# Key-value products of two pairs in one unbroken row of 40 matmuls, and their loads two pairs at a time

## The chip, the cores and the metric

The kernel runs on one core of a Trainium2 chip. The metric is the device time of one execution in microseconds (us), taken as the median of several runs. The granted TensorE clock of the profiled execution is 0.997 of full speed over the whole span.

## What is computed

The reference is a linear attention followed by a gated feed-forward layer, for 8 batches, 8 heads of 64 columns and 576 rows:

```python
kv = np.einsum('bhsd,bhse->bhde', k, v)            # 64 x 64 for each batch and head
out = np.einsum('bhsd,bhde->bhse', q, kv)
rms = np.sqrt(np.mean(out * out, axis=-1, keepdims=True) + 1e-06)
x = out / rms * g_norm                              # heads side by side: 576 x 512
...
h = np.maximum(x @ w_in, 0.0)                       # 576 x 1024, halves u and v
v_n = (v - mu) / np.sqrt(var + 1e-06)
v_s = np.einsum('ts,bsd->btd', w_spatial, v_n) + b_spatial[None, :, None]
out = (u * v_s) @ w_out
```

## The kernel before

Two heads make a pair, so a batch has four pairs (`NP = 4`). For each pair `att_k` makes the key-value product: the 576 rows are four chunks of 128 and a tail of 64 (`NC + 1 = 5`), and for each chunk there is one matmul for either head, whose 64 x 64 result goes to its own half of the partitions. That is a row of 10 matmuls in full fp32. The trace records an fp32 matmul twice, so the row has 20 records there. Each pair has a PSUM tile `pskv` of its own from the pool `ps_att` (three banks). VectorE copies the result of the one head, ScalarE that of the other, into `KVB[p % 2]` (even batches) or `KVO[p]` (odd batches).

The keys and values of a pair lie in one of two buffers, `KV[0]` and `KV[1]`, with the tails in `KT`. `att_load` orders these loads on SyncE's queue, and a buffer is loaded anew when the products that read it are done. The queries (`qt`) and the last 128 queries of odd batches (`qs`) have two buffers each.

`att_q` multiplies four chunks of queries by the pair's `kv` (four matmuls `pso`) and normalizes; the tail rows of all pairs collect in `pst` (`att_end`). `att_t` transposes (`pstr`, for the tail `pstt`), and the result is split in a high and a low fp32r part, `XH` and `XL`.

The feed-forward part of a batch then runs as long streams of fp32r matmuls with three products for each operand pair: `psh` (512 columns), `psu` (288 columns), `psa`, `psb` and `psc` (the spatial product, 288 columns) and `pso2` (the output, 512 columns; the trace drops the digit and calls it `pso`, line 272). Batch 0 and the weights are prepared at the start by the order that is written out in `PLAN`, with plain fp32 products (`L355`, `L379`, `L388`). From batch 2 on, `att_steps` gives a list of attention steps, and the functions `first`, `second` and `last` take one step of it after every piece of feed-forward work of the batch before; the scheduler then places the instructions of each engine.

In `att_steps` the steps of an even batch are `K[0], K[1], Q[0], K[2], Q[1], T[0], K[3], ...` and those of an odd batch begin with `K[0], K[1], K[2], K[3]`.

Of the kernel before, what the change touches and what calls it, by code (L numbers as in the profile page):

```python
# [8 lines left out]
F32 = mybir.dt.float32  # L9
# [7 lines left out]
B, H, S, D = 8, 8, 576, 64  # L17
DM, FF = 512, 1024
FH = FF // 2
P = 128  # L20
NP = H // 2
NC = S // P
# [3 lines left out]
NT = NC * P  # L26
# [6 lines left out]
NB = B  # L33
PLAN = """
N8 W L J00 n6 D00 L n8 W G J01 n6 B00 C A01 L n6 W L J02 T00 H00 H10 D02 C H20 H30 B01 W C J03 T01 Z H01 H11 D03 H21 H31 W C
W B02 L T02 H02 H12 H22 H32 W B03 C W d0 T03 H03 H13 H23 H33 b0 e0 e1 e2 e3 C L K10 C t0 L K11 C
u00 u01 u02 u03 F0 L K12 F1 W W L K13 F2 W W W W d1 b1 F3 u10 Q0 u11 X0 u12 L A10 X1 u13 t1 X2 L B10 A11 h X3
T10 s L B11 E0 T11 s A12 s L B12 E1 z s T12 A13 X4 W s B13 L X5 Q1 s T13 X6 L s X7 s P O0 O1 p R W
"""

# [6 lines left out]
def body(ctx: ExitStack, tc, qT, kvm, kvt, g2, w_in, wsT, bsp, w_out, out):  # L47
    nc = tc.nc
# [11 lines left out]
    def persistent(shape, dt, name):  # L60
        return const.tile(shape, dt, name=name, tag=name)
# [21 lines left out]
    TA = [persistent([P, FH + HF], F32R, f"TA{i}") for i in range(2)]  # L83
    TB = [persistent([P, FH + HF], F32R, f"TB{i}") for i in range(2)]
    U = persistent([P, 4, S], F32, "U")
    KVB = [persistent([P, P], F32, f"KVB{i}") for i in range(2)]
    KVO = [persistent([P, P], F32, f"KVO{i}") for i in range(NP)]


    KV = [persistent([P, 2, NC, P], F32, f"KV{i}") for i in range(2)]  # L90
# [9 lines left out]
    keys, queries = {}, {}  # L100
    n_load = [0]

    def att_load(b, p, kind):
        if kind in "fk":
            kv, kt = (x[n_load[0] % 2] for x in (KV, KT))
            n_load[0] += 1
            for i, j in ((0, 2), (2, NC)) if (b, p) == (0, 0) else ((0, NC),):
                nc.sync.dma_start(kv[:, :, i:j], kvm[b, p, :, :, i:j])
            nc.sync.dma_start(kt[0:TAIL], kvt[b, p])
            keys[b, p] = kv, kt, None  # L110
        if kind == "k":
            qs = load.tile([P, P], F32, name="qs", tag="qs")
            nc.sync.dma_start(qs, qT[b, p, :, S - P:S])
            keys[b, p] = kv, kt, qs
        else:
            n = S if kind == "f" else NT
            qt = load.tile([P, S], F32, name="qt", tag="qt")
            nc.sync.dma_start(qt[:, 0:n], qT[b, p, :, 0:n])
            queries[b, p] = qt

    def att_k(b, p, st, copy=nc.vector.tensor_copy):
        kv, kt, qs = keys.pop((b, p))
        ps = ps_att.tile([P, 512], F32, name="pskv", tag="att")

        for c in range(NC + 1):
            of = kv[:, :, c] if c < NC else kt
            for h in slice(0, D), slice(D, P):
                nc.tensor.matmul(ps[h, h], of[:, 0, h], of[:, 1, h],  # L128
                                 start=c == 0, stop=c == NC)
        st[p] = KVO[p] if b % 2 else KVB[p % 2]  # L130
        copy(st[p][0:D, 0:D], ps[0:D, 0:D])
        nc.scalar.copy(st[p][D:P, D:P], ps[D:P, D:P])
        if qs is not None:
            att_end(p, st, qs)
        issue()

    def att_end(p, st, q):

        if p == 0:
            st["tail"] = ps_tail.tile([P, 512], F32, name="pst", tag="tail")  # L140
        nc.tensor.matmul(st["tail"][:, p * P:(p + 1) * P], q, st[p], start=True, stop=True)  # L141
# [23 lines left out]
    def norm_a(ps, rows=P, accumulate=False):  # L165
        x = work.tile([P, 512], F32, name="x", tag="x")[0:rows]
        ss = small.tile([P, 8], F32, name="ss", tag="ss")[0:rows]
        if accumulate:
            for h in range(8):
                cols = slice(h * D, (h + 1) * D)  # L170
                nc.scalar.activation(x[:, cols], ps[0:rows, cols], AF.Square,
                                     accum_out=ss[:, h:h + 1])
        else:
            nc.scalar.activation(x, ps[0:rows], AF.Square)  # L174
            nc.vector.tensor_reduce(ss, heads(x), axis=AX.X, op=ALU.add)  # L175
        return ps, x, rows, rsqrt_a(ss, 8, rows, 1.0 / D, "h")
# [7 lines left out]
    def att_qa(b, p, st, accumulate=False):  # L184
        qt = queries.pop((b, p))
        ps = ps_att.tile([P, 512], F32, name="pso", tag="att")
        for c in range(NC):
            nc.tensor.matmul(ps[:, c * P:(c + 1) * P], qt[:, c * P:(c + 1) * P], st[p],  # L188
                             start=True, stop=True)
        if b % 2 == 0:  # L190
            att_end(p, st, qt[:, S - P:S])
        issue()
        st[p] = norm_a(ps, P, accumulate)

    def att_qb(b, p, st):
        st[p] = norm_b(*st[p])

    def att_q(b, p, st):
        att_qa(b, p, st)
        att_qb(b, p, st)  # L200

    def tail_a(b, st, accumulate=False):
        st["xt"] = norm_a(st["tail"], P, accumulate)

    def tail_b(b, st):
        st["xt"] = norm_b(*st["xt"])
# [35 lines left out]
    def att_steps(b):  # L242

        st = states.setdefault(b, {})

        def loading(f):
            return lambda: (f(), ahead())

        def t2():
            att_t(b, 2, st)  # L250
            tail_a(b, st)
            tail_b(b, st)

        def tail():
            tail_a(b, st)
            tail_b(b, st)

        K = [lambda p=p: att_k(b, p, st) for p in range(NP)]
        Q = [loading(lambda p=p: att_q(b, p, st)) for p in range(NP)]
        T = [lambda p=p: att_t(b, p, st) for p in range(NP)]  # L260
        end = lambda: att_tail(b, st)
        if b % 2 == 0:
            return [K[0], K[1], Q[0], K[2], Q[1], T[0], K[3], Q[2], T[1], Q[3], t2, T[3], end], []
        return [loading(k) for k in K] + [tail, end], [Q[0], Q[1], T[0], Q[2], T[1], Q[3], T[2],
                                                       T[3], move_tail]


    def three(ps, pairs):
# [135 lines left out]
    def product(ps, q, n, of, start=True, stop=True):  # L404


        cols = slice(q * P, (q + 1) * P)
        pairs = [m for k in range(2) for m in hl(VH[:, k, n, cols], VL[:, k, n, cols],
                                                 WSH[:, k, of], WSL[:, k, of])]
        for i, (lt, rh) in enumerate(pairs):  # L410
            nc.tensor.matmul(ps, lt, rh, start=start and i == 0, stop=stop and i == len(pairs) - 1,  # L411
                             skip_group_check=True)
# [195 lines left out]
    def split_tail():  # L608
# [10 lines left out]
        for n in (TAIL, r):  # L619
            keep(nc.scalar.copy(WTL[1][n - TAIL:n - TAIL + 1], f32(WTL[0][n:n + 1])))  # L620

    todo = [(b + (kind != "f"), p, kind) for b in range(0, B, 2) for kind in "fkq"
            for p in range(NP)]
    states = {}
    wanted = [0]

    def issue():

        while wanted[0] and todo and (len(queries) if todo[0][2] == "q" else len(keys)) < 2:
            wanted[0] -= 1  # L630
            att_load(*todo.pop(0))

    def ahead(n=1):
        wanted[0] += n
        issue()

    nc.vector.memset(KVB[1], 0.0)
    nc.vector.memset(epsc, EPS)
    nc.scalar.activation(small.tile([P, 1], F32, name="warm", tag="av"), epsc, AF.Sqrt)
    nc.gpsimd.memset(KVB[0], 0.0)  # L640
    for kt in KT:
        nc.gpsimd.memset(kt[TAIL:P], 0.0)
    for kvb in KVO:
        nc.gpsimd.memset(kvb, 0.0)
    make_identity(nc, ident)

    def warm(n):

        ps = ps_tail.tile([P, 512], F32, name="psw", tag="tail")
        for _ in range(n):  # L650
            nc.tensor.matmul(ps[:, 0:P], KVB[1], KVB[1], start=True, stop=True)

    def filler(n):
        for _ in range(n):
            tc.keep_in_program_order(
                nc.tensor.matmul(psv[3][:, 0:P], KVB[1], KVB[1], start=True, stop=True))  # L656

    queue = []

# [15 lines left out]
    def outw():  # L675
# [12 lines left out]
    psv = [ps_mm.tile([P, 512], F32, name="psh", tag="mm") for _ in range(NC)]  # L688
    st = [states.setdefault(b, {}) for b in range(2)]
    do = {  # L690
        "N": warm, "n": filler,
        "L": lambda: ahead(), "W": lambda: loads.pop(0)(), "C": lambda: weight64(makes.pop(0)),
        "K": lambda b, p: att_k(b, p, st[b]), "A": lambda b, p: att_qa(b, p, st[b]),
        "B": lambda b, p: att_qb(b, p, st[b]), "T": lambda b, p: att_t(b, p, st[b]),
        "J": lambda b, p: att_k(b, p, st[b], nc.scalar.copy),
        "D": lambda b, p: att_qa(b, p, st[b], True), "d": lambda b: tail_a(b, st[b], True),
        "a": lambda b: tail_a(b, st[b]), "b": lambda b: tail_b(b, st[b]),
        "t": lambda b: att_tail(b, st[b]),
# [3 lines left out]
        "s": lambda: sp_32(*units.pop(0)), "X": split_in, "E": split_ws, "z": split_tail,  # L702
        "Z": blank_tails, "P": outw, "p": gates, "Q": make_out, "O": split_out, "R": split_g,
    }
    for token in PLAN.split():
        do[token[0]](*map(int, token[1:]))

    VH, VL = (vpool.tile([P, 2, 7, HF], F32R, name=f"V{x}", tag=f"V{x}") for x in "HL")

    def first(b):  # L710
# [86 lines left out]
```

## Time and profile before

| what | before |
|---|---|
| time, median of 3 runs | 527.48 us (526.88 to 528.02) |
| the profiled execution's own time | 529.62 us |
| its span, first to last instruction | 527.8 us |
| TensorE matmul busy | 516.2 us, 98% |
| VectorE busy | 360.5 us, 68% |
| ScalarE busy | 241.3 us, 46% |
| key-value products, line 128 | 640 records |

The span is the time that the views of the trace show; 1.8 us of the profiled execution lie around it. A busy share of 98% means that a matmul was in flight, not that the next one began as early as it can: matmuls overlap, so the distance from one start to the next is what counts.

### The profile page before, as it was taken

What the parts mean: (1) busy time and instruction counts of PE and PEld (TensorE: products, weight loads), DVE (VectorE), ACT (ScalarE), POOL (GpSimd) and SP (SyncE); (2) the same over time, 40 slices, a digit from 0 to 9 for tenths busy, and PEclk for the clock granted to TensorE, in tenths of its full rate; (3) what the DMA queues carried; (4) which work ended last, traced back from release to release, by engine and by line L of the source; (5) the groups of instructions that cost most, each with busy time, mean ns of one, the idle gap of its engine ahead of it and who ended that gap; (6) DMA issues with size and microseconds to landing.
All of it is one profiled execution on the core that took longest, in us unless ns stands there. A gap on an engine that the chain in (4) does not pass through costs nothing.

```text
span 527.8 us, 9482 instructions
## 1 busy us (share of the span) xinstructions
PE 516.2 (98%) x3548; PEld 453.8 (86%) x3548; DVE 360.5 (68%) x1089; ACT 241.3 (46%) x629; POOL 9.1 (2%) x25
## 2 busy tenths in 40 slices
PE   7979999999999999999999999999999999999997
PEld 7746867898998899889998899979998889988995
DVE  2887299798792697738693488918586289937480
ACT  2644364875443364435443355324444356334321
POOL 5000000000000000000000000000000000000000
PEclk9989999999999999999999999999999999999999
DMA  8973310251417002021524401020432300010003
GB/s 272 342 259 130 106 42 22 66 196 45 143 31 248 22 2 63 22 81 44 160 64 156 145 21 41 26 81 0 159 108 84 118 21 18 4 69 12 2 2 99
DMA packets 22306, 46.51 MB, mean 88 GB/s; under 512 B 2866, under 2 KB 7474, under 8 KB 22260
## 3 DMA queue, kind: packets, MB, share of 16 engines
q1 hardware_dynamic: 22260, 45.91, 26.8%
q8 instruction: 28, 0.46, 0.4%
q14 instruction: 18, 0.15, 0.1%
HBM read 36.46 MB, written 9.44 MB: 87 GB/s over the span
## 4 chain that ended last, share of the span: by engine, by line
PE 93%; DVE 3%; ACT 1%; DMA 1%; issue 0%; SPq 0%; DVEq 0%
PE pso L272 19%; PE psu L272 17%; PE psh L305 15%; PE psb L411 6%; PE pso L188 5%; PE pskv L128 4%; PE psa L411 4%; PE psc L411 4%; PE psh L355 3%; PE psa L388 3%; PE pstr L216 2%; PE psu L379 2%; PE psh L272 2%; PE psh L656 1%; PE pst L141 1%; DMA KV<-kvm 1%
## 5 line engine op out<-in xcount | busy, mean ns | idle before, releaser
L272 PE MATMUL psu<-XH,WIH 128*128 128x288 f32 x224 | 66.9, 299 | 0.0
L272 PE MATMUL psu<-XL,WIH 128*128 128x288 f32 x224 | 66.1, 295 | 0.0
L272 PE MATMUL psu<-XH,WIL 128*128 128x288 f32 x224 | 66.0, 295 | 0.0
L272 PE MATMUL pso<-WOH,GH 128*128 128x512 f32 x144 | 58.4, 406 | 0.2
L272 PE MATMUL pso<-WOL,GH 128*128 128x512 f32 x144 | 56.6, 394 | 0.0
L272 PE MATMUL pso<-WOH,GL 128*128 128x512 f32 x144 | 54.3, 396 | 0.0
L284 DVE BATCH_NORM_STATS2 s<-v 128x6 f32<-128x512 f32 x32 | 21.9, 691 | 41.6 <-ACT v L278 41.4
L438 ACT CAST GH<-g 128x288 fp32r<-128x288 f32 (+2 forms) x84 | 26.3, 351 | 42.7 <-DVE g L430 42.6
L305 PE MATMUL psh<-WIH,XH 128*128 128x512 f32 x112 | 44.4, 397 | 0.0
L305 PE MATMUL psh<-WIL,XH 128*128 128x512 f32 x112 | 43.7, 390 | 0.0
L305 PE MATMUL psh<-WIH,XL 128*128 128x512 f32 x112 | 43.0, 390 | 0.0
L272 PEld LDWEIGHTS psu<-XH,WIH 128*128 128x128 f32 x224 | 42.0, 188 | 0.7
L272 PEld LDWEIGHTS psu<-XL,WIH 128*128 128x128 f32 x224 | 42.0, 188 | 0.2
L272 PEld LDWEIGHTS psu<-XH,WIL 128*128 128x128 f32 x224 | 42.0, 188 | 0.0
L402 ACT ACTIVATE U<-psu 128x288 f32<-128x288 f32 x56 | 22.9, 410 | 35.4 <-PE psu L272 34.5
L512 ACT COPY o<-pso 128x512 f32<-128x512 f32 x35 | 19.7, 588 | 40.8 <-PE pso L272 36.6
L309 DVE TENSOR_TENSOR VL<-v,VH 128x512 fp32r<-128x512 f32 (+1 forms) x56 | 33.4, 616 | 6.1 <-ACT VH L308 5.7
L175 DVE TENSOR_REDUCE ss<-x 128x8 f32<-128x512 f32 x35 | 23.8, 680 | 16.3 <-ACT x L174 15.9
L308 ACT CAST VH<-v 128x512 fp32r<-128x512 f32 (+1 forms) x56 | 30.3, 564 | 9.5 <-DVE v L331 6.1
L272 PEld LDWEIGHTS pso<-WOH,GL 128*128 128x128 f32 x144 | 27.0, 188 | 5.7
L272 PEld LDWEIGHTS pso<-WOH,GH 128*128 128x128 f32 x144 | 27.1, 188 | 5.5 <-DVE g L430 0.6
L272 PEld LDWEIGHTS pso<-WOL,GH 128*128 128x128 f32 x144 | 27.1, 188 | 4.6
(187 smaller groups left out, 1238.3 us busy)
## 6 DMA issues: line engine op xcount, KB each, us to landing
KV<-kvm SPq DMA_DIRECT2D x31, 512.0 KB, 4.2
out<-o SPq DMA_DIRECT2D x32, 256.0 KB, 2.1
qt<-qT SPq DMA_DIRECT2D x16, 288.0 KB, 2.9
stage<-w_in SPq DMA_DIRECT2D x8, 512.0 KB, 6.6
qt<-qT SPq DMA_DIRECT2D x16, 256.0 KB, 2.7
KT<-kvt SPq DMA_DIRECT2D x32, 64.0 KB, 4.0
stage<-w_out SPq DMA_DIRECT2D x4, 512.0 KB, 3.5
stage<-wsT SPq DMA_DIRECT2D x4, 288.0 KB, 5.0
```

Source lines behind the costliest of these rows:

```text
L128: nc.tensor.matmul(ps[h, h], of[:, 0, h], of[:, 1, h], start=c == 0, stop=c == NC)
L175: nc.vector.tensor_reduce(ss, heads(x), axis=AX.X, op=ALU.add)
L188: nc.tensor.matmul(ps[:, c * P:(c + 1) * P], qt[:, c * P:(c + 1) * P], st[p], start=True, stop=True)
L272: nc.tensor.matmul(ps, lt, rh, start=i == 0, stop=i == n - 1)
L284: nc.vector.bn_stats(s6, v)
L305: nc.tensor.matmul(ps, lt, rh, start=k == 0 and i == 0, stop=k == NP - 1 and i == 2)
L308: nc.scalar.copy(hi, x)
L309: nc.vector.tensor_tensor(lo, x, f32(hi), op=ALU.subtract)
L402: nc.scalar.activation(U[:, d, cols], ps[:, 0:HS], AF.Relu)
L411: nc.tensor.matmul(ps, lt, rh, start=start and i == 0, stop=stop and i == len(pairs) - 1, skip_group_check=True)
L438: nc.scalar.copy(GH[:, d, dst], g[:, src])
L512: nc.scalar.copy(o, ps)
```

## The change

`att_k` takes a tuple of pairs. From batch 1 on it is two pairs, whose 40 records go to one PSUM tile, one after the other, the later pair first; `tc.issue_after` and the raised priority keep them together. One copy on VectorE and one on ScalarE then move both pairs' results, in `KVB` and `KVO` tiles that hold two pairs. Batch 0 keeps a row for each pair (`J`). The list of loads orders keys of two pairs, then queries of two pairs, for even batches from 2 on, and all loads may be ordered as soon as a buffer is free.

```diff
-    def att_k(b, p, st, copy=nc.vector.tensor_copy):
-        kv, kt, qs = keys.pop((b, p))
+    def att_k(b, pairs, st, copy=nc.vector.tensor_copy):
         ps = ps_att.tile([P, 512], F32, name="pskv", tag="att")
-
-        for c in range(NC + 1):
-            of = kv[:, :, c] if c < NC else kt
-            for h in slice(0, D), slice(D, P):
-                nc.tensor.matmul(ps[h, h], of[:, 0, h], of[:, 1, h],
-                                 start=c == 0, stop=c == NC)
-        st[p] = KVO[p] if b % 2 else KVB[p % 2]
-        copy(st[p][0:D, 0:D], ps[0:D, 0:D])
-        nc.scalar.copy(st[p][D:P, D:P], ps[D:P, D:P])
-        if qs is not None:
-            att_end(p, st, qs)
+        to = KVO[pairs[0] // 2] if b % 2 else KVB
+        ends, first = [], None
+
+        def product(p, of, h, c):
+            at = (p - pairs[0]) * P + h
+            return nc.tensor.matmul(ps[h:h + D, at:at + D], of[:, 0, h:h + D], of[:, 1, h:h + D],
+                                    start=c == 0, stop=c == NC)
+
+        for p in reversed(pairs):
+            kv, kt, qs = keys.pop((b, p))
+            for c in range(NC + 1):
+                of = kv[:, :, c] if c < NC else kt
+                for h in (0, D):
+                    if first is None:
+                        first = product(p, of, h, c).ins
+                    else:
+                        with tc.high_priority(), tc.issue_after(first):
+                            product(p, of, h, c)
+            st[p] = to[:, p % 2]
+            ends.append((p, qs))
+        both = ps[:, 0:len(pairs) * P].rearrange("p (j e) -> p j e", e=P)
+        own = slice(p % 2, p % 2 + len(pairs))
+        copy(to[0:D, own, 0:D], both[0:D, :, 0:D])
+        nc.scalar.copy(to[D:P, own, D:P], both[D:P, :, D:P])
+        for p, qs in reversed(ends):
+            if qs is not None:
+                att_end(p, st, qs)
         issue()
...
-            return [K[0], K[1], Q[0], K[2], Q[1], T[0], K[3], Q[2], T[1], Q[3], t2, T[3], end], []
-        return [loading(k) for k in K] + [tail, end], [Q[0], Q[1], T[0], Q[2], T[1], Q[3], T[2],
-                                                       T[3], move_tail]
+            return [K[0], Q[0], Q[1], T[0], K[1], Q[2], T[1], Q[3], t2, T[3], end], []
+        return K + [tail, end], [Q[0], Q[1], T[0], Q[2], T[1], Q[3], T[2], T[3], move_tail]
...
-    todo = [(b + (kind != "f"), p, kind) for b in range(0, B, 2) for kind in "fkq"
-            for p in range(NP)]
+    todo = [(0, p, "f") for p in range(NP)]
+    for b in range(1, B):
+        kinds = ("k", range(NP)), ("q", range(NP))
+        if b % 2 == 0:
+            kinds = [(kind, ps) for ps in ((0, 1), (2, 3)) for kind in "eq"]
+        todo += [(b, p, kind) for kind, ps in kinds for p in ps]
```

What the scheduler makes of it is seen in the order of the instructions on an engine; the line numbers of the changed kernel are its own, and a row's `x` counts instructions, not records.

On TensorE, the first products of batch 6 stood before in four pieces between output matmuls (line 272, `pso_3966` and its like) and `psu` matmuls; these are the first two pieces:

```order
L216 MATMUL pstr<-ident,x 128x128 x4
L128 MATMUL pskv<-KV_101 64x64 x3
L272 MATMUL pso_3982<-WOH,GH 128x512
L272 MATMUL pso_3982<-WOL,GH 128x512
L272 MATMUL pso_3982<-WOH,GL 128x512
L128 MATMUL pskv<-KV_101 64x64 x2
L272 MATMUL pso_3950<-WOH,GH 128x512
```

In the changed kernel the same place on TensorE has both pairs:

```order
L231 MATMUL pstr<-ident,x 128x128 x4
L128 MATMUL pskv<-KV_99 64x64 x8
L128 MATMUL pskv<-KT_101 64x64 x2
L128 MATMUL pskv<-KV_98 64x64 x8
L128 MATMUL pskv<-KT_100 64x64 x2
L422 MATMUL psc<-WSH,VH 128x288
L422 MATMUL psc<-WSL,VH 128x288
```

The 20 matmuls of the two pairs stand together, `KV_99` (the buffer `KV[1]`) ahead of `KV_98`.

On TensorE, batch 1 in the preparation (the part from `J03` on in `PLAN`) stood before like this:

```order
L128 MATMUL pskv<-KV_101 64x64 x8
L128 MATMUL pskv<-KT_103 64x64 x2
L226 MATMUL pstt<-ident,x 128x128 x4
L355 MATMUL psh<-RL,RH 128x512 x4
L128 MATMUL pskv<-KV_102 64x64 x7
L141 MATMUL pst<-KVO_97,qs 128x128
L128 MATMUL pskv<-KV_102 64x64
L128 MATMUL pskv<-KT_104 64x64 x2
L379 MATMUL psu<-RH,RL 128x288 x12
L141 MATMUL pst<-KVO_98,qs 128x128
L379 MATMUL psu<-RH 128x288 x4
```

The same place in the changed kernel, from its second row of products on:

```order
L128 MATMUL pskv<-KV_99 64x64 x8
L128 MATMUL pskv<-KT_101 64x64 x2
L128 MATMUL pskv<-KV_98 64x64 x8
L128 MATMUL pskv<-KT_100 64x64 x2
L390 MATMUL psu<-RH,RL 128x288 x9
L390 MATMUL psu<-RH 128x288 x3
L156 MATMUL pst<-KVO_97,qs 128x128 x2
L390 MATMUL psu<-RH,RL 128x288 x3
L203 MATMUL pso<-KVO_96,qt 128x128 x4
L390 MATMUL psu<-RH,RL 128x288 x9
L390 MATMUL psu<-RH 128x288 x4
L241 MATMUL pstt<-ident,x 128x128 x4
```

The last tail products (`pst`) now stand 16 `psu` and 4 `pso` matmuls ahead of the transposes `pstt` that need them; before, it was 6 `psu` and 4 `pso`.

On SyncE's queue, the loads for batches 4 and 5 stood before as follows (`kvm` and `kvt` are keys and values, `qT` the queries):

```order
L108 DMA KV_101<-kvm 128x1024
L109 DMA KT_103<-kvt 64x256
L108 DMA KV_102<-kvm 128x1024
L109 DMA KT_104<-kvt 64x256
L118 DMA qt<-qT 128x576
L108 DMA KV_101<-kvm 128x1024
L109 DMA KT_103<-kvt 64x256
L118 DMA qt<-qT 128x576
L108 DMA KV_102<-kvm 128x1024
L109 DMA KT_104<-kvt 64x256
```

And now:

```order
L108 DMA KV_99<-kvm 128x1024
L109 DMA KT_101<-kvt 64x256
L108 DMA KV_98<-kvm 128x1024
L109 DMA KT_100<-kvt 64x256
L118 DMA qt<-qT 128x576 x2
L108 DMA KV_99<-kvm 128x1024
L109 DMA KT_101<-kvt 64x256
L108 DMA KV_98<-kvm 128x1024
L109 DMA KT_100<-kvt 64x256
```

Both buffers are now loaded one after the other, behind the same row of products.

## Rows read from the trace of the kernel before

**Rows 1.** The page, part 1: busy time, share of the span and instructions.

```profile
PE 516.2 (98%) x3548; PEld 453.8 (86%) x3548; DVE 360.5 (68%) x1089; ACT 241.3 (46%) x629; POOL 9.1 (2%) x25
```

**Rows 2.** Windows: length, busy time of each engine, granted clock, DMA share, GB/s.

```profile
0.00:66.00 66.00, 58.98 (x397) 43.80 (x398) 39.90 (x120) 29.48 (x130) 7.49 (x22) 0.97 0.67 222
66.00:95.00 29.00, 28.47 (x134) 21.41 (x132) 26.03 (x71) 17.10 (x41) 0.00 (x0) 1.00 0.12 34
95.00:528.00 433.00, 428.75 (x3022) 388.60 (x3020) 294.62 (x899) 194.68 (x460) 1.63 (x3) 1.00 0.22 71
```

**Rows 3.** Timeline of TensorE around one row of 20: start, duration, what.

```profile
246.96 0.29 PE L272 MATMUL psu<-XH,WIL 128*128 128x288 f32 x1
247.18 0.69 PE L128 MATMUL pskv<-KV 128*64 128x64 f32 x16
...
247.91 0.41 PE L272 MATMUL psu<-XH,WIH 128*128 128x288 f32 x1
248.15 0.30 PE L272 MATMUL psu<-XL,WIH 128*128 128x288 f32 x1
...
249.49 0.29 PE L272 MATMUL psu<-XH,WIL 128*128 128x288 f32 x1
```

**Rows 4.** Timeline of TensorE around a row of 40, batch 5.

```profile
289.43 0.40 PE L272 MATMUL pso<-WOL,GH 128*128 128x512 f32 x1
289.75 0.69 PE L128 MATMUL pskv<-KV 128*64 128x64 f32 x16
...
290.38 0.64 PE L128 MATMUL pskv<-KV 128*64 128x64 f32 x16
...
291.07 0.51 PE L272 MATMUL pso<-WOH,GL 128*128 128x512 f32 x1
291.41 0.40 PE L272 MATMUL pso<-WOH,GH 128*128 128x512 f32 x1
...
292.34 0.39 PE L272 MATMUL pso<-WOL,GH 128*128 128x512 f32 x1
```

**Rows 5.** Timeline of TensorE's weight loads at the row of 20.

```profile
247.18 0.55 PEld L128 LDWEIGHTS pskv<-KV 128*64 128x64 f32 x16 [0.16 <-issue]
```

**Rows 6.** Waits of the weight loads from 70 us on: total, times, longest (us).

```profile
PEld pskv L128 <- issue: 4.3, 20, 0.4
PEld pso L272 <- DVE g L430: 0.6, 2, 0.3
```

**Rows 7.** Timeline of TensorE at the tail's transposes of batch 1.

```profile
62.88 0.38 PE L141 MATMUL pst<-KVO,qs 128*128 128x128 f32 x2
...
67.60 0.63 PE L226 MATMUL pstt<-ident,x 128*128 128x128 f32 x4 [0.53 <-DVE qh L152]
```

**Rows 8.** Timeline of VectorE there, with the idle time ahead of it.

```profile
65.08 0.17 DVE L151 TENSOR_SCALAR ah<-ss 128x8 f32<-128x8 f32 x1 [6.97 <-ACT x L171]
```

**Rows 9.** Timeline of all engines at a row of 40, batch 1.

```profile
57.02 0.64 PE L128 MATMUL pskv<-KV 128*64 128x64 f32 x16
...
57.31 0.22 DVE L131 COPY KVO<-pskv 64x64 f32<-64x64 f32 x1 [1.66 <-PE pskv L128]
...
57.71 1.24 PE L379 MATMUL psu<-RH,RL 128*128 128x288 f32 x4
...
58.14 0.21 ACT L132 COPY KVO<-pskv 64x64 f32<-64x64 f32 x1 [0.38 <-DVE KVO L131]
```

**Rows 10.** Timeline of TensorE, batch 3: the starts of its two rows of 40.

```profile
155.35 0.69 PE L128 MATMUL pskv<-KV 128*64 128x64 f32 x16
...
162.52 0.69 PE L128 MATMUL pskv<-KV 128*64 128x64 f32 x16
```

**Rows 11.** Timeline of SyncE between them: the second buffer's tail is ordered.

```profile
157.70 0.47 SPq L109 DMA_DIRECT2D KT<-kvt  x1
```

**Rows 12.** DMA issues from 156 to 158.5 us and over all: median us to landing.

```profile
KT<-kvt SPq DMA_DIRECT2D x2, 64.0 KB, 3.9
...
KV<-kvm SPq DMA_DIRECT2D x31, 512.0 KB, 4.2
```

More of the change, by code (lines that the diff above doesn't have):

```diff
@@ L35 @@
 N8 W L J00 n6 D00 L n8 W G J01 n6 B00 C A01 L n6 W L J02 T00 H00 H10 D02 C H20 H30 B01 W C J03 T01 Z H01 H11 D03 H21 H31 W C
-W B02 L T02 H02 H12 H22 H32 W B03 C W d0 T03 H03 H13 H23 H33 b0 e0 e1 e2 e3 C L K10 C t0 L K11 C
-u00 u01 u02 u03 F0 L K12 F1 W W L K13 F2 W W W W d1 b1 F3 u10 Q0 u11 X0 u12 L A10 X1 u13 t1 X2 L B10 A11 h X3
+W B02 L T02 H02 H12 H22 H32 W B03 C W d0 T03 H03 H13 H23 H33 b0 e0 e1 e2 e3 C L C t0 L K10 C
+u00 u01 u02 u03 F0 L F1 W W L K12 F2 W W W W d1 b1 F3 u10 Q0 u11 X0 u12 L A10 X1 u13 t1 X2 L B10 A11 h X3
 T10 s L B11 E0 T11 s A12 s L B12 E1 z s T12 A13 X4 W s B13 L X5 Q1 s T13 X6 L s X7 s P O0 O1 p R W
@@ L85, in body @@
     U = persistent([P, 4, S], F32, "U")
-    KVB = [persistent([P, P], F32, f"KVB{i}") for i in range(2)]
-    KVO = [persistent([P, P], F32, f"KVO{i}") for i in range(NP)]
+    KVB = persistent([P, 2, P], F32, "KVB")
+    KVO = [persistent([P, 2, P], F32, f"KVO{i}") for i in range(2)]
     KV = [persistent([P, 2, NC, P], F32, f"KV{i}") for i in range(2)]
@@ L103, in att_load @@
     def att_load(b, p, kind):
-        if kind in "fk":
+        if kind in "fek":
             kv, kt = (x[n_load[0] % 2] for x in (KV, KT))
@@ L114, in att_load @@
             keys[b, p] = kv, kt, qs
-        else:
-            n = S if kind == "f" else NT
+        if kind in "fq":
+            n = NT if b % 2 else S
             qt = load.tile([P, S], F32, name="qt", tag="qt")
@@ L244, in att_steps @@
         st = states.setdefault(b, {})
-        def loading(f):
-            return lambda: (f(), ahead())
         def t2():
@@ L256, in tail @@
             tail_b(b, st)
-        K = [lambda p=p: att_k(b, p, st) for p in range(NP)]
-        Q = [loading(lambda p=p: att_q(b, p, st)) for p in range(NP)]
+        K = [lambda p=p: att_k(b, (p, p + 1), st) for p in (0, 2)]
+        Q = [lambda p=p: att_q(b, p, st) for p in range(NP)]
         T = [lambda p=p: att_t(b, p, st) for p in range(NP)]
@@ L635, in ahead @@
         issue()
-    nc.vector.memset(KVB[1], 0.0)
+    nc.vector.memset(KVB[:, 1], 0.0)
     nc.vector.memset(epsc, EPS)
     nc.scalar.activation(small.tile([P, 1], F32, name="warm", tag="av"), epsc, AF.Sqrt)
-    nc.gpsimd.memset(KVB[0], 0.0)
+    nc.gpsimd.memset(KVB[:, 0], 0.0)
     for kt in KT:
@@ L650, in warm @@
         for _ in range(n):
-            nc.tensor.matmul(ps[:, 0:P], KVB[1], KVB[1], start=True, stop=True)
+            nc.tensor.matmul(ps[:, 0:P], KVB[:, 1], KVB[:, 1], start=True, stop=True)
     def filler(n):
@@ L655, in filler @@
             tc.keep_in_program_order(
-                nc.tensor.matmul(psv[3][:, 0:P], KVB[1], KVB[1], start=True, stop=True))
+                nc.tensor.matmul(psv[3][:, 0:P], KVB[:, 1], KVB[:, 1], start=True, stop=True))
     queue = []
@@ L692, in body @@
         "L": lambda: ahead(), "W": lambda: loads.pop(0)(), "C": lambda: weight64(makes.pop(0)),
-        "K": lambda b, p: att_k(b, p, st[b]), "A": lambda b, p: att_qa(b, p, st[b]),
+        "K": lambda b, p: att_k(b, (p, p + 1), st[b]), "A": lambda b, p: att_qa(b, p, st[b]),
         "B": lambda b, p: att_qb(b, p, st[b]), "T": lambda b, p: att_t(b, p, st[b]),
-        "J": lambda b, p: att_k(b, p, st[b], nc.scalar.copy),
+        "J": lambda b, p: att_k(b, (p,), st[b], nc.scalar.copy),
         "D": lambda b, p: att_qa(b, p, st[b], True), "d": lambda b: tail_a(b, st[b], True),
@@ L706, in body @@
         do[token[0]](*map(int, token[1:]))
+    ahead(len(todo))
     VH, VL = (vpool.tile([P, 2, 7, HF], F32R, name=f"V{x}", tag=f"V{x}") for x in "HL")
```

## The prediction, made before the changed kernel ran

> **What bounds the kernel now.** I read the page's busy shares first: TensorE's matmuls are busy for 98% of the span, VectorE for 68%, ScalarE for 46% [rows 1]. Then the windows: from 95 us to the end TensorE is busy 428.75 of 433 us, the rest being the drain at the end, and the clock is at its full level [rows 2]. Up to 66 us, where weights and batch 0 are made ready, it has 7 us of gaps, and from 66 to 95 us VectorE is nearly full too, 26.03 of 29 us. Last the waits: behind 70 us the weight loads wait for another engine only twice, 0.6 us in all, at the head of an output stage [rows 6]. So in 460 of 528 us time goes only where TensorE starts fewer or cheaper matmuls, and the distance between starts is what I price.
>
> **What a row of products costs.** Around a row of 20 records the last `psu` ahead starts at 246.96 and the second one behind at 248.15, 1.19 us later [rows 3]. A `psu` of this stream starts every 0.134 us (248.15 to 249.49 is ten steps), so two steps would have been 0.27: the row costs 0.92 us. Around a row of 40 the same two marks are 289.43 and 291.41, 1.98 us apart; the output stream steps by 0.2325 (291.41 to 292.34, four steps), two steps are 0.465, and the row costs 1.52 [rows 4]. Two rows of 20 cost 1.84, one of 40 costs 1.52: **every row that ceases to stand alone gives back about 0.33 us**, though no matmul is dropped. The view shows where it lies. Weight loads of the stream run ahead of the matmuls, but that of the row's first product waits 0.16 us [rows 5], so its start comes 0.22 instead of 0.134 behind the one before: 0.09. From the row's start to the next matmul's it is 0.73 for 20 and 1.32 for 40, so twice 20 is 0.14 more. And the first matmul behind takes 0.24 instead of 0.134 until the next starts: 0.10. Sum 0.33.
>
> **How many rows go.** Counted in the order of the instructions, batches 1 to 7 had 25 unbroken rows or pieces of rows, and have 14 now, two a batch, each of 40. Behind 95 us it is 21 before and 12 after (the weight loads of `pskv` waited 20 times behind 70 us, [rows 6], so nearly every row paid). The four rows of batch 0 stay. The odd batches 3, 5 and 7 already had two rows of 40 each; what goes is in the even batches, where each pair stood by itself and batches 2 and 6 had one cut in two and four pieces, and in batch 1. Eleven rows fewer at 0.33 are **3.6 us**. Low end: the 0.10 of the first matmul behind falls out where small fp32 work follows rather than a stream, 11 x 0.23 = 2.5 us; I take 0.33, since before the change nearly all of these rows lie inside streams of 288 or 512 columns.
>
> **The preparation.** TensorE stood idle 0.53 us ahead of the tail's transposes `pstt` at 67.60, 4.7 us behind the start of the last `pst` at 62.88 [rows 7]; what it waited for was ScalarE and VectorE normalizing the tail. Now 16 `psu` and 4 `pso` lie between instead of 6 and 4. The ten `psu` more are some 4.9 us by the 62.88 to 67.60 stretch's own matmuls (4.7 less the wait is 4.2 for six `psu`, four `pso` and the `pst`, about half a microsecond a `psu`). So that wait should go: **0.5 us**. Will VectorE, full from 66 us on, keep TensorE from using it? It was idle for 6.97 us up to 65.08 because the tail's sums came late [rows 8], and the earlier `pst` lets it start earlier too. I count the 0.5 whole; the low end is nothing.
>
> **Copies.** Batches 1 to 7 have 14 copies on VectorE and 14 on ScalarE instead of 28 and 28, each of twice the columns; a copy of one pair is 0.22 and 0.21 us [rows 9], so the most that it can save is 3 us on either engine over the span, and neither is the bound: nothing. The first pair's result comes later: before, VectorE's copy of the first pair started at 57.31 while the second pair's matmuls ran from 57.02 to 57.71 in another bank; now it comes behind all 40. ScalarE's copy of the second pair ended at 58.35, 0.64 us behind the row's end, and that is when both will be there. The nearest reader in the new order is a `pso` of batch 4, 18 matmuls of 288 columns behind its row, 2.4 us. So this is hidden; uncovered it would cost up to 0.6 us a row.
>
> The Trainium skill (PSUM — Partial Sum Buffer, section Summary: rules for kernel authors) says that what reads PSUM while a matmul runs should go to a different bank, which speaks against two pairs in one. The trace agrees as far as the copy beside the running matmul was indeed in another bank; by the rule the change gives up that overlap, 14 x 0.6 = 8 us at most, and by the distance to the readers it gives up nothing.
>
> **Loads.** A row now needs both buffers. In batch 3 the two rows started 7.17 us apart [rows 10], and the second buffer's last load was ordered at 157.70 [rows 11]. With 3.9 us to landing in that stretch, 4.2 over all [rows 12], it is there 6.3 to 6.6 us behind the first row's start. Between the two rows of batch 5 the new order has 22 output matmuls where there were 23, so the second row comes about 0.2 us sooner, and its second half, which reads the buffer loaded last, 0.6 us (290.38 less 289.75) behind its start: at 7.6. A margin of about 1 us, so nothing. In even batches the rows are further apart. On SyncE's queue the loads of both buffers stand behind the same row, and what they were moved past (queries, output stores) is ordered at most one row later; the stores that follow there belong to outputs finished later, so I see no store held up.
>
> **The sum.** 3.6 + 0.5 = 4.1 us. The profiled execution would go from a span of 527.8 to 523.7, and from its own 529.62 to 525.5; it lies 2.1 above the median of the runs, which I leave as it is: 527.48 - 4.1 = **523.4 us**.
>
> **The rivals.**
>
> *Partly given back.* TensorE, 4 us quicker, runs into VectorE. For it: the two waits for `g` at the head of an output stage show that the chain behind the last spatial product already just fails to be in time [rows 6], and adjacent steps `Q[0]`, `Q[1]` put two normalizations on VectorE in a row. Against it: 68% busy behind 95 us. If the preparation gives nothing (0.5, and the two rows there, 0.7) and the heads of six output stages wait 0.3 us instead of two, 1.2 more, 1.7 us are left: 525.8.
>
> *The gain is lost to the loads: no change.* The unbroken row cannot let other matmuls pass while it waits. If the later load lands 1.8 instead of about 1 us later than reckoned, the second rows of batches 1, 3, 5 and 7 wait 0.8 us each, 3.2 us: 526.6 or so. For it: both are ordered at once with stores beside them. Against it: 4.2 us is the median of all 31 loads of keys and values, and before the change the rows of the odd batches stood under the same two loads and no wait of `pskv` for a DMA is among those behind 70 us.
>
> *Slower.* The same mechanism further on: from about 1.3 us of wait at each of these four rows on (landings of 6.5 us), 5.2 us outweigh the 4.1, and the time is above 528.5. Nothing in the profile behind 95 us comes near.
>
> *That the change does not do what it says* is excluded by the order: all 14 rows are whole.
>
> **Chances and range.** The forecast, 522.2 to 524.5, has 0.60: the upper end has 0.23 for a row and a little of the 0.5, the lower end adds the two waits for `g`, 0.6 us, and the scatter of the runs, half a microsecond. Partly given back has 0.25, no change 0.10, slower 0.05. This kernel's measurement tells about 0.2% from no change, 1.05 us, so faster means below 526.4: 0.60 + 0.25 = 0.85; same 0.10; slower 0.05. For eight in ten the range runs from 522.2 to 526.4, which leaves out no change, slower and the far ends.
>
> **What would show it.** Right: 14 rows of 40 records behind batch 0, each about 1.32 us from its start to the next matmul's; the windows behind 95 us some 3 us shorter with TensorE's busy share unchanged; no wait ahead of `pstt`. Wrong: `pskv` waiting for a DMA in the odd batches; more or longer waits for `g` or `XL` at the heads of stages; a first matmul behind a row that takes as long as any other, in which case the price of a row was not the row's.

## The result, and the profile after

The changed kernel takes 522.62 us (median of 6 runs, 521.54 to 524.77). The kernel before took 527.66 us in the same session (6 runs, 526.88 to 529.48). The ratio is 0.9904, with a 95% interval of 0.9879 to 0.9929. The change gives 5.0 us where 4.1 were forecast. In three later sessions the same kernel gave ratios of 0.9923, 0.9899 and 0.9933, or 3.7, 5.6 and 3.7 us by the medians. Four single executions of the later sessions, which took 732 to 2912 us, are left out of every median here.

The profiled execution took 521.54 us. The page's first part answers to [rows 1]:

```profile
PE 507.7 (98%) x3548; PEld 450.0 (87%) x3548; DVE 360.0 (69%) x1075; ACT 240.1 (46%) x615; POOL 8.5 (2%) x23
```

TensorE has as many instructions as before and is busy for the same share. VectorE and ScalarE have lost 14 copies each, and 0.5 and 1.2 us of busy time: TensorE still bounds the kernel.

The two spans, 527.8 and 519.7 us, differ by more than the medians do, so I cut them at three matmuls that both have in the same place: the transposes of the last pair of batch 0 in the preparation (`T03` in `PLAN`), the first fp32r `psh`, and the last output matmul. The timeline of TensorE before:

```profile
41.52 0.60 PE L216 MATMUL pstr<-ident,x 128*128 128x128 f32 x4
...
94.90 0.61 PE L305 MATMUL psh<-WIH,XH 128*128 128x512 f32 x1
...
523.53 0.39 PE L272 MATMUL pso<-WOH,GL 128*128 128x512 f32 x1
```

And after:

```profile
38.42 0.60 PE L231 MATMUL pstr<-ident,x 128*128 128x128 f32 x4
...
90.45 0.61 PE L316 MATMUL psh<-WIH,XH 128*128 128x512 f32 x1
...
515.41 0.39 PE L283 MATMUL pso<-WOH,GL 128*128 128x512 f32 x1
```

| stretch | before | after | difference |
|---|---|---|---|
| start, up to the first mark | 41.52 | 38.42 | -3.10 |
| preparation, first to second mark | 53.38 | 52.03 | -1.35 |
| streams, second to third mark | 428.63 | 424.96 | -3.67 |

The preparation and the streams together lost 5.02 us, as much as the two medians above differ by. They are steadier than the medians: the three later profiles of the changed kernel have 477.1, 477.1 and 477.5 us for the two together, after 477.0 in the first, and 482.0 before. The start differs from execution to execution of one kernel (last section); up to the first mark TensorE, VectorE and ScalarE have the same instructions and SyncE the same loads, in the same order, before and after. From here on "preparation" and "streams" mean these two stretches.

A row of 40 in a stream of `psu`, as TensorE's timeline shows it after the change:

```profile
242.15 0.29 PE L283 MATMUL psu<-XH,WIL 128*128 128x288 f32 x1
242.37 0.69 PE L128 MATMUL pskv<-KV 128*64 128x64 f32 x16
...
243.68 0.40 PE L283 MATMUL psu<-XH,WIH 128*128 128x288 f32 x1
243.92 0.29 PE L283 MATMUL psu<-XL,WIH 128*128 128x288 f32 x1
```

From 242.15 to 243.92 it is 1.77 us. Two steps of 0.134 would be 0.27, so the row costs 1.50, about what the row of 40 cost before [rows 4]. It holds the products that cost 1.84 us as two rows of 20 [rows 3].

The waits of the weight loads from 70 us on (total, times, longest) answer to [rows 6]:

```profile
PEld pskv L128 <- issue: 1.3, 8, 0.2
PEld psh L316 <- DVE XL L225: 0.5, 1, 0.5
PEld pso L203 <- ACT KVB L146: 0.3, 1, 0.3
```

Four things have changed. The waits ahead of `pskv` fell from 20 to 8. The two waits for `g` are gone. Two new waits stand there, for `XL` and for `KVB`, once each. And a wait in the preparation is gone that [rows 6] leave out, though the same view before has it:

```profile
PEld psa L388 <- DVE U L390: 0.4, 1, 0.4
```

It stood at 83.97. The 16 records of `psa` from 81.93 to 86.01 took 4.08 us before, and take 3.89 now (77.67 to 81.56), so it cost 0.19. No `pskv` waits for a DMA.

The waits for `g` stood at the head of two output stages. TensorE's timeline at the first of them, before:

```profile
337.76 0.30 PE L419 MATMUL psb<-WTL,TB 128*128 128x288 f32 x1
338.13 0.50 PE L272 MATMUL pso<-WOH,GH 128*128 128x512 f32 x1
338.47 0.39 PE L272 MATMUL pso<-WOL,GH 128*128 128x512 f32 x1
```

The same place after:

```profile
330.00 0.29 PE L430 MATMUL psc<-WTL,TB 128*128 128x288 f32 x1
330.14 0.39 PE L283 MATMUL pso<-WOH,GH 128*128 128x512 f32 x1
330.37 0.40 PE L283 MATMUL pso<-WOL,GH 128*128 128x512 f32 x1
```

From the first to the third row it was 0.71 us, and is 0.37 now. Such a wait cost 0.34 us, and two of them 0.7.

The new waits stand in batch 2. All engines' timeline there, after:

```profile
101.47 0.68 DVE L574 SCALAR_TENSOR_TENSOR stage<-stage,t 128x512 f32<-128x512 uint32 x1
...
102.07 0.75 DVE L225 SCALAR_TENSOR_TENSOR XL<-pstr,gcol,XH 128x512 fp32r<-128x512 f32 x1
...
102.42 0.39 PE L316 MATMUL psh<-WIL,XH 128*128 128x512 f32 x1
...
102.87 1.21 PE L316 MATMUL psh<-WIH,XL 128*128 128x512 f32 x4
103.33 0.27 DVE L145 COPY KVB<-pskv 64x128 f32<-64x128 f32 x1
...
103.64 0.26 ACT L146 COPY KVB<-pskv 64x128 f32<-64x128 f32 x1 [1.38 <-DVE KVB L145]
...
103.95 0.97 PEld L203 LDWEIGHTS pso<-KVB,qt 128*128 128x128 f32 x8 [0.31 <-ACT KVB L146]
```

VectorE is still splitting `w_out` there (`stage`, line 574). `XL` and the copy of the row's result stand in its queue behind that, and ScalarE's copy stands behind VectorE's. The `psh` at 102.87 comes 0.45 us behind the one before, where a step is 0.23, and the `pso` comes 1.08 behind four `psh`, which take 0.93: 0.22 and 0.15, together 0.37 us, are lost.

In the preparation nothing waits ahead of `pstt` any more. TensorE's timeline from the last `pst` to it answers to [rows 7]:

```profile
54.28 0.61 PE L156 MATMUL pst<-KVO,qs 128*128 128x128 f32 x4
...
63.38 0.60 PE L241 MATMUL pstt<-ident,x 128*128 128x128 f32 x4
```

It is 9.1 us from the last `pst` to `pstt`, where it was 4.7, and the row carries no wait.

### The profile page after: what moved, and what is told of

Same layout as the page of the kernel before. It is cut to its first block, busy times and chain, and to the rows that moved or that the text cites. A ratio compares the mean times of both kernels' runs of the same rounds, so it can differ in the third digit from the quotient of the medians.

```text
span 519.7 us, 9439 instructions
## 1 busy us (share of the span) xinstructions
PE 507.7 (98%) x3548; PEld 450.0 (87%) x3548; DVE 360.0 (69%) x1075; ACT 240.1 (46%) x615; POOL 8.5 (2%) x23
## 4 chain that ended last, share of the span: by engine, by line
PE 86%; DMA 5%; DVE 4%; ACT 3%; issue 1%; SPq 0%; DVEq 0%
PE pso L283 19%; PE psu L283 17%; PE psh L316 13%; PE psb L422 6%; PE pso L203 4%; PE psc L422 4%; PE psa L422 4%; PE pskv L128 4%; DMA KV<-kvm 3%; PE psu L390 3%; PE pstr L231 2%; PE psh L366 2%; PE psh L283 2%; PE pst L156 1%; DMA KT<-kvt 1%; DVE WSL L580 1%
## 5 line engine op out<-in xcount | busy, mean ns | idle before, releaser
L283 PE MATMUL pso<-WOH,GH 128*128 128x512 f32 x144 | 57.1, 398 | 0.0
```

The costliest lines, as they stand in the source:

```text
L283: nc.tensor.matmul(ps, lt, rh, start=i == 0, stop=i == n - 1)
```

## The experiments

Theory A is that of the prediction: each row that stands alone costs, by what TensorE pays on either side of it. Theory B: the gain came from the loads, which may now be ordered earlier, or from the joint copies. Theory C: most of it is the start, which differs between executions. Each experiment was timed beside the kernel before in its session. The changed kernel was run again in each session; its streams took 424.96 us in the first and 425.03, 425.12 and 425.44 in the later ones.

The change also has a new `PLAN`, which the excerpt of its diff leaves out: `K11` and `K13` are gone, since `K10` and `K12` now make two pairs each, and the tail of batch 0 (`t0`) stands ahead of `K10` instead of behind it. `e5_loads` has the old `PLAN`, the other experiments have the new one.

### The changed kernel again, and a foreign matmul between or ahead of the pairs

`r0_again` is the changed kernel itself.

> The changed kernel once more, as the mark for the other runs on the same chip. Theory A (a separate row of products costs TensorE about 0.33 us): 14 rows of 40, and from the first fp32r psh matmul to the last matmul 425.0 us again, within 0.3, whatever the start does. Rival B (the loads and the shorter list of attention steps gave the gain): the same. Rival C (a good part of the gain is luck of the start: the clock granted early and loads landing early): the stretch up to the first fp32r psh, 90.5 us in the first profile, differs by more than 1 us between executions of this one kernel.

In `e1_between` one fp32 matmul of 128 columns with weights of 128 x 128 stands in the middle of each of the 14 rows. Its result is not used.

```diff
+        def extra():
+            return nc.tensor.matmul(ps[:, 256:384], ident, ident, start=True, stop=True)
...
         for p in reversed(pairs):
+            if len(pairs) > 1 and p == pairs[0]:
+                with tc.high_priority(), tc.issue_after(first):
+                    extra()
```

> One extra fp32 matmul of the identity with itself (128 columns of weights) stands between the two pairs of each of the 14 rows, so every row of 40 is two of 20; its result is not used. Against the run with the same matmul ahead of the row: theory A expects 14 x 0.33 = 4.6 us more over all, and 12 x 0.33 = 4.0 more from the first fp32r psh to the last matmul; rival B expects no difference, 0.3 us or less, since loads, list and copies are the same.

In `e2_ahead` the same matmul stands ahead of the row, which stays whole. In batches 1, 3, 5 and 7 the scheduler moved that of the second row further ahead, in 3, 5 and 7 beside that of the first row; TensorE's work is the same.

```diff
+        if len(pairs) > 1:
+            first = extra().ins
```

> The same extra matmul, result not used, ahead of the first product of each of the 14 rows, which stay whole. Both theories expect the extra matmul's own time alone, about 0.22 us each by the step of 0.11 us a record: 12 x 0.22 = 2.7 us more than the changed kernel from the first fp32r psh to the last matmul.

In `e3_half` it stands in the middle again, but has weights of 64 columns, as the products have.

```diff
-            return nc.tensor.matmul(ps[:, 256:384], ident, ident, start=True, stop=True)
+            return nc.tensor.matmul(ps[0:D, 256:384], ident[:, 0:D], ident, start=True, stop=True)
```

> Between the two pairs of each row stands an extra fp32 matmul with 64 columns of weights and 128 moving columns, result not used: an interruption as in the run with the extra matmul between, but with weights of the products' own width. If what a separate row pays is the change of the weights' width, the row goes on unbroken, no weight load waits and the whole costs no more than the run with the matmul ahead (2.7 us over the changed kernel behind the first fp32r psh, or less). If any interruption costs the same, it is as slow as the run with the full matmul between, 4.0 us above that.

| kernel | median us | ratio, interval | preparation | streams |
|---|---|---|---|---|
| r0_again | 523.51 | 0.9923 (0.9900 to 0.9945) | 52.02 | 425.03 |
| e1_between | 530.93 | 1.0065 (1.0030 to 1.0099) | 53.15 | 431.50 |
| e2_ahead | 525.88 | 0.9977 (0.9954 to 1.0000) | 52.46 | 427.69 |
| e3_half | 526.31 | 0.9982 (0.9960 to 1.0003) | 52.43 | 427.49 |

By the two stretches the same matmul costs 4.5 us more between the pairs than ahead of them, 0.32 for each of the 14 rows; the medians differ by 5.05. One row of each in TensorE's timeline shows where. `e1_between`, matmul in the middle:

```profile
246.86 0.29 PE L289 MATMUL psu<-XH,WIL 128*128 128x288 f32 x1
247.08 0.69 PE L128 MATMUL pskv<-KV 128*64 128x64 f32 x16
...
247.81 0.49 PE L132 MATMUL pskv<-ident 128*128 128x128 f32 x2
248.23 0.69 PE L128 MATMUL pskv<-KV 128*64 128x64 f32 x16
...
248.96 0.40 PE L289 MATMUL psu<-XH,WIH 128*128 128x288 f32 x1
```

`e2_ahead`, matmul ahead:

```profile
245.60 0.29 PE L288 MATMUL psu<-XH,WIL 128*128 128x288 f32 x1
245.73 0.38 PE L132 MATMUL pskv<-ident 128*128 128x128 f32 x2
246.05 0.69 PE L128 MATMUL pskv<-KV 128*64 128x64 f32 x16
...
247.36 0.41 PE L288 MATMUL psu<-XH,WIH 128*128 128x288 f32 x1
```

`e3_half`, matmul in the middle with weights of 64 columns:

```profile
244.67 0.29 PE L289 MATMUL psu<-XH,WIL 128*128 128x288 f32 x1
244.89 0.69 PE L128 MATMUL pskv<-KV 128*64 128x64 f32 x16
...
245.52 0.28 PE L132 MATMUL pskv<-ident 128*64 128x128 f32 x1
...
246.42 0.40 PE L289 MATMUL psu<-XH,WIH 128*128 128x288 f32 x1
```

From the `psu` ahead to the `psu` behind it is 1.53 us in the changed kernel (242.15 to 243.68), 2.10 in e1, 1.76 in e2 and 1.75 in e3: between the pairs the matmul costs 0.34 more than ahead of them, if its weights have 128 columns, and nothing more if they have 64. So a foreign matmul in the middle costs no more than one ahead, provided that its weights are as wide as those of the products (`128*64` in the row). What a row that stands alone pays is thus the change between weights of 128 and of 64 columns, once on either side, and not that something stands between its halves. That goes beyond theory A as it was predicted. The matmul of e3 also writes only half of the partitions, as each product does; whether the weights' width or this counts was not told apart. The Trainium skill (TensorEngine Tiling (Array Packing), Tiling Modes, Key Properties) says that changing the tiling mode, and not just the tile, drains TensorE. These rows agree: the matmul costs 0.57 us in e1, where the row's `128*64` becomes `128*128`, and 0.22 in e3, where it stays.

### Undoing one part at a time

`e4_free` is the changed kernel without the lines that hold a row together:

```diff
-                        with tc.high_priority(), tc.issue_after(first):
-                            product(p, of, h, c)
+                        product(p, of, h, c)
```

> The changed kernel without the two lines that keep a row together (the raised priority and the order behind its first matmul), so that the scheduler may cut the rows of 40; tiles, copies, steps and loads are those of the change. By the order of the instructions there are 24 rows and pieces instead of 18, 16 instead of 12 of them behind the preparation. If a row that stands alone is what costs (0.33 us each): from the first fp32r psh to the last matmul 4 x 0.33 = 1.3 us more than the changed kernel's 425.0, so 426.3, two more in the preparation, and some 2.0 us in all, about 525.4 at a median of 523.5 for the changed kernel. If the joint copies or the new loads brought the gain, however the products stand: as the changed kernel, 425.0 and about 523.5.

`e5_loads` is the kernel before with the change's loads alone:

```diff
-    todo = [(b + (kind != "f"), p, kind) for b in range(0, B, 2) for kind in "fkq"
-            for p in range(NP)]
+    todo = [(0, p, "f") for p in range(NP)]
+    for b in range(1, B):
...
+        todo += [(b, p, kind) for kind, ps in kinds for p in ps]
...
+    ahead(len(todo))
```

> The kernel before with only the new list of loads, all of them allowed as soon as a buffer is free; rows, copies and steps as before, 21 rows and pieces behind the preparation. If rows are what costs: as the kernel before, 428.6 us from the first fp32r psh to the last matmul, about 527.3 in all, within 0.2%. If the earlier loads brought the gain: as the changed kernel, 425.0 and about 523.5.

`e8_single` is the changed kernel with one pair to a step from batch 2 on:

```diff
-        K = [lambda p=p: att_k(b, (p, p + 1), st) for p in (0, 2)]
+        K = [lambda p=p: att_k(b, (p,), st) for p in range(NP)]
...
-            return [K[0], Q[0], Q[1], T[0], K[1], Q[2], T[1], Q[3], t2, T[3], end], []
+            return [K[0], K[1], Q[0], K[2], Q[1], T[0], K[3], Q[2], T[1], Q[3], t2, T[3], end], []
```

> The changed kernel with loads, tiles and the preparation as they are, but with the products of one pair a step, and a copy of its own on either engine for each pair, in batches 2 to 7 (steps K0, K1, Q0, K2, Q1 and so on, as before the change). 23 rows instead of 18, 17 instead of 12 behind the preparation. If rows are what costs: 5 x 0.33 = 1.65 us more, 426.7 us from the first fp32r psh to the last matmul and about 525.2 in all at 523.5 for the changed kernel; if the doubled number of copies mattered as well, up to 3 us more on VectorE, and then the waits of TensorE for XL or g must rise; if neither, 425.0 and about 523.5.

`r1_again` is the changed kernel, timed beside these three.

> The changed kernel once more beside the other three: 523.5 us, 425.0 us from the first fp32r psh to the last matmul.

| kernel | median us | ratio, interval | preparation | streams |
|---|---|---|---|---|
| r1_again | 521.92 | 0.9899 (0.9881 to 0.9916) | 52.01 | 425.12 |
| e8_single | 524.84 | 0.9949 (0.9928 to 0.9969) | 52.02 | 427.37 |
| e4_free | 527.24 | 0.9994 (0.9974 to 1.0015) | 54.50 | 426.83 |
| e5_loads | 527.33 | 1.0014 (0.9999 to 1.0030) | 53.40 | 428.60 |

The loads alone give nothing: e5 has the two stretches of the kernel before to 0.03 us. Theory B falls for the loads by themselves; a joint row needs both pairs' loads early, and what it would cost under the old list was not tried.

e8 lost more than the 1.65 us of its five rows: 2.25 in the streams. One of the waits of its weight loads from 70 us on says why:

```profile
PEld pso L283 <- DVE g L441: 0.6, 2, 0.3
```

Both waits for `g` are back, 0.7 us by the timeline above, and the wait for `KVB`, 0.15, is gone: 1.65 and 0.7 less 0.15 are 2.2. e4, which keeps the change's list of attention steps but cuts rows, has no wait for `g`. So these two waits belong to the list of steps, not to the rows as such: VectorE's timeline of e8 has an `XL` of 0.70 us at 332.29, between the `g` at 331.44 and that at 333.79, and that of the changed kernel has none at this place. That this `XL` is what makes `g` late is read from the timeline and was not tried. Next to nothing is left over for the copies, of which e8 has twice as many in batches 2 to 7, so theory B falls for them too, unless it is the copies that make `g` late.

e4 lost 1.7 us in the streams, with four more pieces (1.3 forecast). The waits for `XL` and `KVB` are gone there too, and a weight load of `psu` waits 0.8 us for `v` instead; the loss was not divided further. That the rest of its loss is in the preparation was not foreseen, and one row of its timeline on TensorE names the place:

```profile
67.81 0.63 PE L240 MATMUL pstt<-ident,x 128*128 128x128 f32 x4 [1.18 <-DVE qh L172]
```

There the last `pst` ran at 62.70, and `pstt` waits 1.18 us, where the kernel before waited 0.53 [rows 7]. A scheduler that may cut the rows puts back the late tail too, although `PLAN` is that of the change. So without the two lines that hold a row together the preparation loses all of its gain and 1.1 us more, and the streams lose nearly half of theirs. Of e4's 2.5 us in the preparation the wait is 1.2, and two pieces at 0.33 would be 0.7; the rest was not divided.

### Taking the new waits away

The 0.37 us lost in batch 2 looked like a gain still to be had. Three kernels move one step of `PLAN`, so that VectorE takes `XL` and the copy ahead of splitting `w_out`. In `n1_early`:

```diff
-T10 s L B11 E0 T11 s A12 s L B12 E1 z s T12 A13 X4 W s B13 L X5 Q1 s T13 X6 L s X7 s P O0 O1 p R W
+T10 s L B11 E0 T11 s A12 s L B12 E1 z s T12 A13 X4 W s B13 L T13 X5 Q1 s X6 L s X7 s P O0 O1 p R W
```

> The changed kernel with one step of the preparation moved in PLAN: T13, the transposes of the last pair of batch 1 and their split in XH and XL, stands ahead of X5, so that on VectorE XL and the copy of the first row of batch 2 come ahead of the splitting of the last quarter of w_out. If what the changed kernel gives back at 102.9 to 104 us (a weight load 0.5 us for XL, then one 0.3 us for KVB) is that VectorE stands in splitting weights there, both waits go and the time is 0.8 us less than the changed kernel's, 424.2 from the first fp32r psh to the last matmul or the preparation as much shorter. If VectorE's work as a whole is the bound there, the wait moves to another place of the first 130 us and the time stays within 0.3 us of the changed kernel's.

`n2_mid` has `L X5 T13 Q1 s X6` there:

> As n1_early, but T13 one step later, behind X5 and ahead of Q1. The same two outcomes: 0.8 us less than the changed kernel if the order of VectorE's work is what makes XL and KVB late, within 0.3 us of it if VectorE's work as a whole is.

`n3_before` has `L X5 s T13 X6 L s X7 s P Q1 O0 O1`:

> T13 stays where it is and Q1, which makes that quarter of w_out, goes behind the s and P that follow. The same two outcomes: 0.8 us less than the changed kernel if the order of VectorE's work is what makes XL and KVB late, within 0.3 us of it if VectorE's work as a whole is.

`r2_again` is the changed kernel, timed beside these three.

> The changed kernel beside the other three: 522 to 523.5 us, 425.0 us from the first fp32r psh to the last matmul, 52.0 us for the preparation.

| kernel | median us | ratio, interval | preparation | streams |
|---|---|---|---|---|
| r2_again | 523.77 | 0.9933 (0.9909 to 0.9957) | 52.02 | 425.44 |
| n1_early | 529.07 | 1.0022 (1.0006 to 1.0038) | 52.02 | 431.40 |
| n2_mid | 527.46 | 0.9989 (0.9971 to 1.0008) | 52.02 | 430.64 |
| n3_before | 528.23 | 1.0006 (0.9985 to 1.0027) | 52.02 | 429.51 |

Neither outcome came. The waits for `XL` and `KVB` are gone in all three, and one wait some ten times as long has taken their place, 4.2, 3.5 and 3.6 us. That of n1 among its weight loads' waits from 60 us on:

```profile
PEld psu L283 <- ACT U L413: 4.2, 1, 4.2
```

ScalarE's timeline of n1 there:

```profile
113.03 2.39 ACT L319 CAST GH<-U 128x576 fp32r<-128x576 f32 x4 [1.46 <-DVE WOL L320]
115.32 0.66 ACT L319 CAST WOH<-stage 128x512 fp32r<-128x512 f32 x1
115.89 0.99 ACT L413 ACTIVATE U<-psu 128x288 f32<-128x288 f32 x3
```

The `U` that `psu` waits for stands in ScalarE's queue behind four casts `GH`, which waited 1.46 us for VectorE's `w_out` work (`WOL`), and a cast `WOH`. TensorE's timeline of n1 at that place:

```profile
112.08 0.29 PE L283 MATMUL psu<-XH,WIL 128*128 128x288 f32 x1
116.33 0.61 PE L283 MATMUL psu<-XH,WIH 128*128 128x288 f32 x1 [3.97 <-ACT U L413]
116.74 0.44 PE L283 MATMUL psu<-XL,WIH 128*128 128x288 f32 x1
...
122.02 0.44 PE L283 MATMUL psu<-XH,WIL 128*128 128x288 f32 x1
122.26 0.34 PE L283 MATMUL psu<-XH,WIH 128*128 128x288 f32 x1
```

The wait is not all of it. Behind it a `psu` starts every 0.24 us (116.74 to 122.02 is 22 steps) instead of every 0.134, until 122.26. The windows of n1 (length, busy TensorE, granted clock, DMA share, GB/s) say why:

```profile
104.00:112.00 8.00, 8.00 (x62) 1.00 0.58 177
112.00:116.00 4.00, 0.36 (x3) 0.94 0.00 0
116.00:122.00 6.00, 5.67 (x23) 0.50 0.27 87
```

The granted clock is 0.50, the lower of its two levels, for the 6 us that follow the idle 4 us. From 116.33 to 122.26 there are 24 steps, 5.93 us instead of 3.22: 2.7 us more. With 4.1 for the wait and 0.4 saved that makes 6.4 lost, and the streams lost 5.96. None of the three beats the changed kernel.

## Why the prediction was right

**What bounds the kernel.** Right: TensorE's busy share stayed at 98%, and the distance between its starts was the right measure.

**What a row costs.** Right in mechanism and in size. The row of 40 costs 1.50 us in a `psu` stream, where the prediction took 1.52 from an output stream; two rows of 20 cost 1.84 there, so a row less is 0.34. e1 against e2 gives 0.32 to 0.34 for a row that is cut in two. The cause was put down to the row's edges, and e3 made it narrower: the change of the weights' width. The first matmul behind the row takes 0.24 until the next (243.68 to 243.92), as in [rows 3].

**How many rows go.** Right: 14 rows of 40 stand behind batch 0, 12 of them in the streams instead of 21. One reading was wrong without changing the count: not every pair of the even batches stood by itself before, for batch 2 began with a row of 40 (at 103.84). The streams lost 3.67 us. Of these 0.7 are the waits for `g`, and 0.37 were given back to `XL` and `KVB`, so by subtraction 3.3 are left for the nine rows. At 0.34 they gave 3.1; the other 0.3 is not traced to a place.

**The preparation.** Right: 1.35 us, where two rows at 0.33 and the 0.53 ahead of `pstt` make 1.2. The rest is the wait of `psa` for `U`, 0.19. The prediction read [rows 6] as all waits for another engine behind 70 us, and this one is missing from them. TensorE could use the gain, though VectorE is nearly full there.

**The step that was mis-sized** is the sum, which left out the waits for `g`. The prediction knew them [rows 6], and put them in the low end of the range and, the other way round, in a rival in which they become six. They vanished with the new list of attention steps (e8, e4). Between the 4.1 forecast and the 5.0 found that is 0.7 more; the rows at 0.34 and the 0.3 not traced add 0.4, the wait of `psa` 0.2, and the new waits take 0.37. That the sum was too low is read from the stretches. The medians do not settle it: their differences in the four sessions, 3.7 to 5.6, lie on both sides of 4.1, and the forecast time, 523.4, lies within the 521.9 to 523.8 of the four.

**Copies.** Nearly right. At most places nothing waits for them. In batch 2 a weight load waits 0.31 us for `KVB`, and the cause is not the one weighed in the prediction: the copies come late because VectorE's queue is full of `w_out`, not because both pairs share a bank. Of the 8 us that the prediction names as the most that sharing could cost, nothing shows.

**Loads.** Right: no `pskv` waits for a DMA in the streams, and e5 shows that their order by itself is worth nothing.

**The rivals.** "Partly given back" happened at one place, with 0.37 us, and was outweighed. "No change" and "slower" did not happen. Of theory C this is left: the start accounts for 3.1 of the 8.1 us by which the spans differ, so that pair of profiles read without marks would have overstated the gain.

## What to carry to other kernels

Price a small piece of TensorE work by the distance between the starts of its neighbours, not by its busy time; where its weights have another width than the stream's, that distance holds a fixed part, here about 0.34 us, which is saved by putting such pieces together and not by dropping any. Before adding up a forecast, look at every wait that lies within a microsecond of the moved steps, since a new order may remove it or make it, and write the price of both into the sum. Cut two profiles at instructions that they share before comparing spans.

## What was not expected of the hardware

The change of weights' width is what costs: weights of 64 columns put in the middle of a row cost 0.22 us (e3), weights of 128 columns 0.57 (e1), and 0.23 ahead of it (e2).

In n1 one idle time of about 4 us on TensorE, at full clock before it, was followed by about 6 us at the lower clock level, so that 4.1 us of waiting cost 6.8. In n2 and n3 idle times of 3.3 and 3.4 us were followed by 5.5 and 3.0 us in which a `psu` started every 0.24 us.

The start of one and the same program differs. The first mark of the changed kernel lay at 38.42, 39.62, 38.42 and 40.08 us in its four profiles, so runs of one kernel differ by more than a microsecond for a reason that lies ahead of everything the change touches. In the profile before, the clock was low for a part of the start. Its window from 28 to 34 us:

```profile
28.00:34.00 6.00, 5.22 (x11) 0.72 0.89 298
```

And after:

```profile
28.00:34.00 6.00, 5.12 (x22) 1.00 0.89 290
```

In the other twelve profiles this window has 1.00 too. What the low clock cost is seen in one row of the chain that ended last, before:

```profile
29.29 5.40 PE psh L355 x8
```

In e5, which has the old `PLAN` and the same start, these eight records took 3.70 us at full clock, 1.7 less, and the first mark came at 40.00 instead of 41.52. About half of the 3.1 us by which the two starts differ is thus this clock. TensorE had been idle for 0.80 and 0.78 us shortly before; in e5 it was idle for as long there, and the clock stayed at 1.00. Why it fell in the one and not in the others stays open.
